# Products of zeros in an attention opening, and another order of loads, transposes and scores for four chunks

## The chip, the cores and the metric

The kernel runs on one core of one Trainium2 chip. The metric is the device time of one execution in microseconds (us), here the median over runs; lower is better. The engines are named as in the profile: PE (TensorE, matrix products), PEld (its weight loads), DVE (VectorE), ACT (ScalarE), POOL (GpSimd) and SP (SyncE, which issues most transfers).

## What is computed

A linear attention with decay over blocks of 64 tokens, whose output goes through a two-layer network. For each batch, head and block:

```python
intra = einsum('bhij,bhjd->bhid', einsum('bhic,bhjc->bhij', qb, kb) * Dmask, vb)
inter = einsum('bhid,bhde->bhie', qb * lam_pow, kv_state)
out[:, :, sl] = intra + inter
kv_state = lam_block * kv_state + einsum('bhsd,bhse->bhde', kb * rev_pow, vb)
...
x = out.transpose(0, 2, 1, 3).reshape(3072, 512)
h = x @ w_in                      # 512 x 2048
return (h / (1 + exp(-h))) @ w_out  # 2048 x 512
```

There are 4 batches, 8 heads, 768 tokens and head size 64; inputs and outputs are float32, and the products are made in bfloat16.

## The kernel before

**Chunks and groups.** The 3072 tokens are cut into 24 chunks of 128 (two blocks of 64 for all 8 heads), two chunks to a group of 256 tokens. A chunk needs q, k and v from memory, scaled by powers of the decay and cast (`prep` on POOL for q and k, `vcast` on ACT for v), then q and k transposed. From chunk 6 on the transposes are made by DMA (`dma_t`, lines 390 and 391), two for each chunk, issued by SP; loads are issued by SP as well (`load_1`, line 232), so both stand in one queue in the order of the program.

**The opening.** Chunks 0 to 3 and the first layer for groups 0 and 1 follow an order written out by hand (`ORDER`), one word for one step: `kc`, `qc`, `vc` scale and cast (last letter: D for DVE, A for ACT, P for POOL); `tk`, `tq` are transposes on PE and `kt`, `qt` copy them out; `s` is the scores, `m` their mask on DVE, `d` the product that adds to the state, `kv` the state's copy to bfloat16, `i` and `o` the two parts of the attention's output, `x` its copy out; `w` casts a piece of w_in, `u` is a part of the first layer and `g` its Silu. Steps of one engine run in the order of the words. `z:n` stands for products of zeros, n units of 256 columns: as long as the state's tile (tag `kv`) isn't open, `op_z` makes them at once, into a tile of the same tag; later it only notes n, for the next tile that `zeros` is called with.

**The groups.** After a middle part for groups 0 and 1, a loop over groups g = 2 to 10 has two stages. First come eight units of the first layer (`ffn1_two`, 8 products of 256 columns each, then a Silu on ACT; two banks of tag `h`, so a unit waits for the Silu two units before it). Then come eight units of the second layer (`downs`, 4 products of 512 columns each; four units make one output of 128 tokens, which DVE copies out, line 648). Two banks `o0` and `o1` take the outputs in turn; `other()` names the one that is not in use by the present output. Between units stand the steps of later chunks: `preps`, `transposes`, `load_qk`, `load_vs`, `vcast`, and `section`, which makes outputs, scores and states of two chunks on PE and lets DVE mask the scores (line 560), add to the state (572) and cast it. In the loop c, d, a, b are the chunks 2g + 2 to 2g + 5. At unit 6 of the second stage a section makes the outputs of c and d and the scores and states of a and b. For chunks 8 and 9 the scores and states were made in a section of their own, ahead of the first layer's last unit in group 3:

```python
if g == 3 and i == 7:
    section((), (c, d), steps(c, d))
ffn1_two(g, i)
```

The loads of q and k ran one chunk ahead of those of v (`c + 7`, `d + 7`), and v of 10 and 11 was issued by ACT (`e=nc.scalar`).

Of the kernel before, what the change touches and what calls it, by code (L numbers as in the profile page):

```python
# [7 lines left out]
F32 = mybir.dt.float32  # L8
# [4 lines left out]
BLK = 128  # L13
# [7 lines left out]
LOADS = "K00 Q00 K01 Q01 V00 V01 K20 Q20 K21 Q21 V20 V21"  # L21

ORDER = """
wl kc:0,0,D,u z:20 qc:0,0,D tk:0,0,o tq:0,0,att kc:0,1,D,s kt:0,0,A qc:0,1,D z:4 qt:0,0,A tk:0,1,h s:0,0,h,o
vc:0,0,P,s kt:0,1,A tq:0,1,att m:0,0,0,D qc:2,0,P vc:0,1,D,u qt:0,1,A s:0,1,h,att kc:2,0,A,u d:0 m:0,0,1,D kv:0,A
tk:2,0,o i:0,0,att,h kt:2,0,A d:1 m:0,1,1,D kv:1,A o:0,0 x:0,0,A m:0,1,0,D vc:2,0,P,s x:1,0,A kc:2,1,D,s tq:2,0,o
tk:2,1,h qt:2,0,D qc:2,1,D s:2,0,o,att m:2,0,0,D i:0,1,o,att tq:2,1,h m:2,0,1,D o:0,1 vc:2,1,D,u d:2,0 kt:2,1,A
qt:2,1,A s:2,1,h,o kv:2,0,A i:2,0,att,att x:0,1,A d:2,1 m:2,1,0,D m:2,1,1,D kv:2,1,A w:0,0,A w:0,1,D o:2,0 i:2,1,h,h
x:2,0,D d:3 o:2,1 x:1,1,D x:3,0,A u:0,0,0,o,o x:3,1,A u:1,0,0,att,att w:1,0,D x:2,1,D w:2,1,D w:1,1,A w:2,0,D w:3,0,D
# [7 lines left out]
def kernel(  # L37
# [10 lines left out]
    nc = tc.nc  # L48
    B, H, S, D = q.shape
# [4 lines left out]
    NP = H // 2  # L54
# [14 lines left out]
    psum = ctx.enter_context(tc.tile_pool(name="psum", bufs=1, space=bass.MemoryType.PSUM))  # L69
# [40 lines left out]
    zero = const.tile([128, 512], BF16, name="zero")  # L110
# [84 lines left out]
    natb, tr, st, kvb, kvps = {}, {}, {}, {}, {}  # L195
    xts = []
    cell = {}

    def zeros(dst):
        fill(dst, cell.pop("z", 0))  # L200

    def fill(dst, n):
        dst = dst if len(dst.shape) == 2 else dst.rearrange({3: "p a b -> p (a b)", 4: "p a b c -> p (a b c)", 5: "p a b c d -> p (a b c d)"}[len(dst.shape)])
        w = dst.shape[1] // 256
        for k in [w] * (n // w) + [1] * (n % w):
            nc.tensor.matmul(dst[:, 0:256 * k], lhsT=zero[:, :BLK], rhs=zero[:, 0:256 * k], start=True, stop=True, skip_group_check=True)
    start = 0
    group_of = {}
    for g, n in enumerate(GROUPS):
# [28 lines left out]
    def load_v(c, e=None):  # L238
        vraw[c] = load_1(v, c, "vf", 6, e)
# [15 lines left out]
    kp, vp, qp, qtp, ktp, sp_, ss_, op_ = {}, {}, {}, {}, {}, {}, {}, {}  # L255
# [25 lines left out]

    def op_s(c, a, *tags):
        sps = [psum.tile([128, 2, 2, 2, 64], F32, name="sp", **bank(t)) for t in tags]
        zeros(sps[0])
        for r in range(2):
            for p in range(2):
                for j, x in ((0, 0), (1, 1), (0, 1), (1, 0)):
                    nc.tensor.matmul(sps[j][half[x], r, p], lhsT=ktp[c][half[j], 2 * a + p, r, half[x]],
                                     rhs=qtp[c][half[j], 2 * a + p, :, half[x]], start=True, stop=True)
        sp_[c, a] = sps  # L290
# [15 lines left out]
    def op_i(c, a, *tags):  # L306
        for x, t in enumerate(tags):
            op_[c + x, a] = psum.tile([128, 2, 2, 64], F32, name="op", **bank(t), padded_shape=[128, NP, 2, 64])
        zeros(op_[c, a])
        last = {}  # L310
        for x, j in ((0, 1), (1, 0), (0, 0), (1, 1)) if c else ((1, 0), (1, 1)):
            for p in range(2):
                last[j] = nc.tensor.matmul(op_[c + x, a][half[j], p], lhsT=kvb[c + x][half[j], 2 * a + p, :],
                                           rhs=qtp[c][half[j], 2 * a + p, :, half[x]], start=(p == 0), stop=False,
                                           skip_group_check=True)
        cell["i", c, a] = list(last.values())
# [18 lines left out]
    def op_d(c, a=None):  # L335
        c0, x = c - c % 2, c % 2
        if c == 0:
            kvps[0] = psum.tile([128, NP, D], F32, name="kv_ps", tag="kv", bufs=1, padded_shape=[128, NP, BLK])
        kv = kvps[0]
        for r in range(2):  # L340
            for p in range(NP) if a is None else (2 * a, 2 * a + 1):
                for j in range(2):
                    h = 2 * (p % 2) + j
                    nc.tensor.matmul(kv[half[j], p, :], lhsT=kp[c0][half[x], p // 2, r, h, :],
                                     rhs=vp[c0][half[x], p // 2, r, h, :],
                                     start=(c == 0 and r == 0 and p == 0), stop=True, skip_group_check=True)
# [248 lines left out]
    hps = {}  # L595

    def ffn1_open(g, i, tag="h"):
        hps[g, i] = psum.tile([128, 512], F32, name="h_ps", **bank(tag))

    def ffn1_mm(g, i, kos):  # L600
        for u in range(2):
            m, a = 2 * i + u, 256 * u
            for ko in kos:
                nc.tensor.matmul(hps[g, i][:, a:a + 256], lhsT=w_in_bf[:, ko, m * 128:(m + 1) * 128], rhs=xt[g][:, ko, :],  # L604
                                 start=(ko == 0 and u == 0), stop=(ko == KO_IN - 1), skip_group_check=True)
# [68 lines left out]
    for word in LOADS.split():  # L674
        a = int(word[2])
        src, dst = {"Q": (q, rawq), "K": (k, rawk), "V": (v, vraw)}[word[0]]
# [5 lines left out]
    def op_u(g, b, h, *tags):  # L682
        if b == 0:
            for i, tag in enumerate(tags):
                ffn1_open(g, i, tag)
            if h == 0:
                zeros(hps[g, 0])
            for i in range(2):
                ffn1_mm(g, i, range(2 * h, 2 * h + 2))
            return  # L690
        ms = (4 * b + 2 * g, 4 * b + 2 * g + 1)
        for m, tag in zip(ms, tags):
            hps["m", m] = psum.tile([128, 512], F32, name="h_ps", **bank(tag))
        if h == 0:
            zeros(hps["m", ms[0]])
        for m in ms:
            for ko in range(2 * h, 2 * h + 2):
                nc.tensor.matmul(hps["m", m], lhsT=w_in_bf[:, ko, m * 128:(m + 1) * 128], rhs=xall[0][:, :, ko, :],  # L698
                                 start=(ko == 0), stop=(ko == KO_IN - 1))
# [13 lines left out]

    def op_z(n):
        if 0 in kvps:
            cell["z"] = n
        else:
            wt = psum.tile([128, NP, BLK], F32, name="warm_ps", tag="kv", bufs=1)
            fill(wt, n)

    table = {
        "qc": op_c(rawq, qp, "qb2", True), "kc": op_c(rawk, kp, "kp"), "vc": op_c(vraw, vp, "vp"),
# [4 lines left out]
    for word in ORDER.split():  # L727
        name, _, args = word.partition(":")
# [6 lines left out]
    def load_qk(*cs, e=None):  # L735
        for c in cs:
            if c < NCHUNK:
                rawq[c] = load_1(q, c, "qf", 4, e)
                load_k(c, e)
                loaded.append(c)  # L740

    def transposes(*cs):
        for c in cs:
            if c < NCHUNK:
                dma_t(c)

    def load_vs(*cs, e=None):
        for c in cs:
            if c < NCHUNK:
                load_v(c, e)  # L750

    def preps(*cs):
        for c in cs:
# [49 lines left out]
    def steps(*cs):  # L803
        return [(c, h) for c, h in [(cs[0] - 1, 1)] + [(c, h) for c in cs for h in range(2)] if c > 5][:-1]

    many = (("h", 2),) * 2 + (("att", 3),) * 2
    for g in range(2, len(GROUPS) - 1):
        c, d, a, b = range(2 * g + 2, 2 * g + 6)
        for i in range(8):
            if g == 2 and i == 4:  # L810
                preps(8, 9)
                load_qk(10)
                transposes(8, 9)
                load_vs(8, 9)
                load_qk(11)
            if g < 4 and i in (4, 5):
                vcast(c + i % 2)
            if g == 3 and i == 7:
                section((), (c, d), steps(c, d))
            ffn1_two(g, i)  # L820
        for i, unit in enumerate(downs(g)):
            if i == 1 and g == 2:
                section((), (c, d), steps(c, d))
            if i == 1 and g > 2:
                vcast(a)
            if i == 2:
                preps(c + 4, d + 4)
                transposes(c + 4, d + 4)
                load_qk(*([12] if g == 2 else []), c + 7)
                load_vs(c + 6, d + 6)  # L830
                load_qk(d + 7)
            if i == 3 and g > 2:
                vcast(b)
            if i == 0 and g == 2:
                load_vs(10, 11, e=nc.scalar)
            if i == 6:
                cs = [x for x in (a, b) if g > 2 and x < NCHUNK]
                section((c, d), cs, steps(*cs) if cs else (), "AD", many[:2] if cs else many, other())
            ffn2(*unit)
    g = len(GROUPS) - 1  # L840
# [35 lines left out]
```

## Time and profile before

| | |
|---|---|
| median of 3 runs | 204.93 us (204.31 to 205.45) |
| the profiled execution | 205.49 us |
| its span, first to last instruction | 203.8 us |
| mean granted PE clock | 0.99 |
| PE busy | 196.6 us (96%) |
| DVE, ACT, POOL busy | 81.5, 90.0, 53.5 us |

All starts below are in us from the first instruction of the profiled execution. A busy PE is not PE at its peak, since products are pipelined; a wait is put down to the work that ended last before it. The granted clock is the share of full speed that PE was given.

### The profile page before, as it was taken

What the parts mean: (1) busy time and instruction counts of PE and PEld (TensorE: products, weight loads), DVE (VectorE), ACT (ScalarE), POOL (GpSimd) and SP (SyncE); (2) the same over time, 40 slices, a digit from 0 to 9 for tenths busy, and PEclk for the clock granted to TensorE, in tenths of its full rate; (3) what the DMA queues carried; (4) which work ended last, traced back from release to release, by engine and by line L of the source; (5) the groups of instructions that cost most, each with busy time, mean ns of one, the idle gap of its engine ahead of it and who ended that gap; (6) DMA issues with size and microseconds to landing.
All of it is one profiled execution on the core that took longest, in us unless ns stands there. A gap on an engine that the chain in (4) does not pass through costs nothing.

```text
span 203.8 us, 6077 instructions
## 1 busy us (share of the span) xinstructions
PE 196.6 (96%) x2636; PEld 130.5 (64%) x2636; DVE 81.5 (40%) x176; ACT 90.0 (44%) x165; POOL 53.5 (26%) x98
## 2 busy tenths in 40 slices
PE   7689999999999899999999999999999999999994
PEld 2368444557747656856856856856856856856854
DVE  1897357294072085515315415414315415412011
ACT  3864973454704731641641641741741741622610
POOL 5240002657062126434425153440400000000000
PEclk9969999999999999999999999999999999999999
DMA  4999999999679949849789594997997601101102
GB/s 107 336 369 408 400 408 270 279 266 211 148 151 164 239 80 246 194 83 227 162 187 201 116 264 91 226 215 169 269 384 152 245 2 55 53 3 55 51 2 103
DMA packets 95579, 38.67 MB, mean 190 GB/s; under 512 B 80960, under 2 KB 88512, under 8 KB 95552
## 3 DMA queue, kind: packets, MB, share of 16 engines
q1 hardware_dynamic: 91248, 37.24, 70.5%
q10 hardware_dynamic: 4304, 1.05, 3.1%
q8 instruction: 20, 0.33, 0.7%
q14 instruction: 7, 0.06, 0.1%
HBM read 27.27 MB, written 6.29 MB: 165 GB/s over the span
## 4 chain that ended last, share of the span: by engine, by line
PE 64%; DMA 2%; SPq 1%; ACT 1%; issue 0%; POOL 0%; DVE 0%
PE o_ps L642 29%; PE h_ps L604 28%; PE op L540 3%; DMA vf<-in_v_dram 2%; PE o_part L662 2%; PE sp L540 1%; SPq L391 1%; PE kv_ps L540 1%; ACT vb L178 0%; POOL kb L364 0%; ACT g L609 0%; DVE ob L182 0%; SPq L390 0%
## 5 line engine op out<-in xcount | busy, mean ns | idle before, releaser
L642 PE MATMUL o_ps<-w_out_bf,g 128*128 128x512 bf16 x368 | 83.8, 379 | 0.0
L604 PE MATMUL h_ps<-xt,w_in_bf 128*128 128x256 bf16 x672 | 75.7, 273 | 1.0 <-ACT g L609 1.0
L604 PEld LDWEIGHTS <-w_in_bf 128*128 128x128 bf16 x672 | 65.6, 98 | 11.2 <-issue 1.1
L609 ACT ACTIVATE g<-h_ps 128x512 bf16<-128x512 f32 x84 | 49.9, 597 | 41.3 <-PE h_ps L604 41.0
L642 PEld LDWEIGHTS <-g 128*128 128x128 bf16 x368 | 34.8, 98 | 38.3
L178 ACT ACTIVATE xt<-op 128x256 bf16<-128x256 f32 (+1 forms) x18 | 8.3, 487 | 46.9 <-issue 34.4
L364 POOL TENSOR_TENSOR qb<-qf,lam_fwd 128x256 bf16<-128x256 f32 x18 | 11.3, 625 | 59.7 <-issue 31.3
L648 DVE COPY ob<-o_ps 128x512 f32<-128x512 f32 x11 | 7.6, 689 | 46.6 <-PE o_ps L642 46.6
L560 DVE TENSOR_TENSOR ss<-sp,mask 128x512 bf16<-128x512 f32 x20 | 12.8, 682 | 14.9 <-PE sp L540 14.9
L182 DVE CAST xt<-op 128x256 bf16<-128x256 f32 (+1 forms) x16 | 8.3, 543 | 21.2 <-PE op L540 20.1
L648 DVE COPY pair<-o_ps 128x512 f32<-128x512 f32 x12 | 8.2, 686 | 16.5 <-PE o_ps L642 16.5
L572 DVE TENSOR_TENSOR total<-total,kv_ps 128x256 f32<-128x256 f32 x33 | 13.6, 414 | 0.1
L364 POOL TENSOR_TENSOR kb<-kf,lam_bwd 128x256 bf16<-128x256 f32 x20 | 12.4, 618 | 4.6 <-DMA kf<-in_k_dram 3.4
L365 POOL TENSOR_TENSOR kb<-kf,lam_bwd 128x256 bf16<-128x256 f32 x20 | 12.5, 625 | 0.0
L178 ACT ACTIVATE vb<-vf 128x512 bf16<-128x512 f32 x20 | 11.6, 622 | 0.9 <-DMA vf<-in_v_dram 0.9
L365 POOL TENSOR_TENSOR qb<-qf,lam_fwd 128x256 bf16<-128x256 f32 x18 | 11.2, 620 | 0.0
L182 DVE CAST kvs<-total 128x256 bf16<-128x256 f32 x33 | 10.5, 319 | 1.1
L698 PE MATMUL h_ps<-xt,w_in_bf 128*128 128x512 bf16 x48 | 10.5, 379 | 0.0
L540 PEld LDWEIGHTS <-vb 64*64 64x64 bf16 x320 | 7.5, 105 | 4.5 <-issue 4.2
L540 PE MATMUL op<-ss,vb 64*64 64x64 bf16 x320 | 9.9, 199 | 0.0
L540 PE MATMUL op<-qt,kvs 64*64 64x64 bf16 x296 | 9.6, 194 | 0.0
L698 PEld LDWEIGHTS <-w_in_bf 128*128 128x128 bf16 x48 | 4.7, 98 | 5.4
(76 smaller groups left out, 126.2 us busy)
## 6 DMA issues: line engine op xcount, KB each, us to landing
kf<-in_k_dram SPq DMA_DIRECT2D x19, 256.0 KB, 4.5
vf<-in_v_dram SPq DMA_DIRECT2D x18, 256.0 KB, 4.2
qf<-in_q_dram SPq DMA_DIRECT2D x17, 256.0 KB, 4.0
pair<-in_moe_w_out_dram SPq DMA_DIRECT2D x8, 512.0 KB, 7.8
pair<-in_moe_w_in_dram SPq DMA_DIRECT2D x6, 512.0 KB, 7.3
out_dram<-pair SPq DMA_DIRECT2D x12, 256.0 KB, 3.9
out_dram<-ob SPq DMA_DIRECT2D x11, 256.0 KB, 3.8
pair<-in_k_dram SPq DMA_DIRECT2D x4, 256.0 KB, 4.5
```

What stands on the lines that cost most here:

```text
L178: nc.scalar.activation(dst, src, AF.Copy)
L182: nc.vector.tensor_copy(dst, src)
L364: eng.tensor_tensor(dst[:, 0::2], src[:, 0::2, ::-1, :], by[:, 0::2, ::-1, :], op=AL.mult)
L365: eng.tensor_tensor(dst[:, 1::2], src[:, 1::2], by[:, 1::2], op=AL.mult)
L540: ins = nc.tensor.matmul(dst, lhsT=lhsT, rhs=rhs, start=start, stop=True, skip_group_check=True)
L560: nc.vector.tensor_tensor(ss, sp.rearrange("k w p q -> k (w p) q"), mask64[:, None, :].to_broadcast([128, len(scores) * NP, D]), op=AL.mult)
L572: nc.vector.tensor_tensor(total[b], old, place(c, h), op=AL.add)
L604: nc.tensor.matmul(hps[g, i][:, a:a + 256], lhsT=w_in_bf[:, ko, m * 128:(m + 1) * 128], rhs=xt[g][:, ko, :], start=(ko == 0 and u == 0), s ...
L609: nc.scalar.activation(gg.rearrange("p u n -> p (u n)"), hps[g, i], AF.Silu)
L642: nc.tensor.matmul(o, lhsT=gt[g, ko][:, mt * BLK:(mt + 1) * BLK], rhs=w_out_bf[:, ko, :], start=(ko == 0), stop=(ko == KO_OUT - 1))
L648: nc.vector.tensor_copy(ob, o)
L698: nc.tensor.matmul(hps["m", m], lhsT=w_in_bf[:, ko, m * 128:(m + 1) * 128], rhs=xall[0][:, :, ko, :], start=(ko == 0), stop=(ko == KO_IN - 1))
```

## The change

Three things are changed.

- In the opening, `z:20` becomes `z:22`, a `z:6` is put ahead of the first transpose of q (`tq:0,0`), a `z:6` ahead of the second scores (`s:0,1`), and a `z:4` ahead of the first transpose of k of chunk 2 (`tk:2,0`). The old `z:4` stays between `tq:0,0` and `tk:0,1`. For the last of them `op_z` is changed: once the state's tile is open, it makes the products at once, 256 columns each and adding, into the second half of that tile, which is now allocated at the same size with two halves.
- In group 2, the loads of v of 8 and 9, q and k of 11, and v of 10 and 11 all stand ahead of the transposes of 8 and 9, and SP issues them; the transposes of 10 and 11 then follow with no loads between. From there each group loads q, k and v of its two chunks after the transposes of the two before (`c + 6`, `d + 6`).
- The section for the scores of 8 and 9 is moved from ahead of unit 7 of the first layer in group 3 to ahead of unit 2 of the second layer.

```diff
-wl kc:0,0,D,u z:20 qc:0,0,D tk:0,0,o tq:0,0,att kc:0,1,D,s kt:0,0,A qc:0,1,D z:4 qt:0,0,A tk:0,1,h s:0,0,h,o
-vc:0,0,P,s kt:0,1,A tq:0,1,att m:0,0,0,D qc:2,0,P vc:0,1,D,u qt:0,1,A s:0,1,h,att kc:2,0,A,u d:0 m:0,0,1,D kv:0,A
-tk:2,0,o i:0,0,att,h kt:2,0,A d:1 ...
+wl kc:0,0,D,u z:22 qc:0,0,D tk:0,0,o z:6 tq:0,0,att kc:0,1,D,s kt:0,0,A qc:0,1,D qt:0,0,A z:4 tk:0,1,h s:0,0,h,o
+vc:0,0,P,s kt:0,1,A tq:0,1,att m:0,0,0,D qc:2,0,P vc:0,1,D,u qt:0,1,A z:6 s:0,1,h,att kc:2,0,A,u d:0 m:0,0,1,D kv:0,A
+z:4 tk:2,0,o i:0,0,att,h kt:2,0,A d:1 ...
...
-    def zeros(dst):
-        fill(dst, cell.pop("z", 0))
-
-    def fill(dst, n):
...
+    def fill(dst, n, start=True):
         w = dst.shape[1] // 256
         for k in [w] * (n // w) + [1] * (n % w):
-            nc.tensor.matmul(dst[:, 0:256 * k], lhsT=zero[:, :BLK], rhs=zero[:, 0:256 * k], start=True, stop=True, skip_group_check=True)
+            nc.tensor.matmul(dst[:, 0:256 * k], lhsT=zero[:, :BLK], rhs=zero[:, 0:256 * k], start=start, stop=True,
+                             skip_group_check=True)
...
         if c == 0:
-            kvps[0] = psum.tile([128, NP, D], F32, name="kv_ps", tag="kv", bufs=1, padded_shape=[128, NP, BLK])
+            both = psum.tile([128, 2, NP, D], F32, name="kv_ps", tag="kv", bufs=1)
+            kvps[0], cell["spare"] = both[:, 0], both[:, 1].rearrange("k p d -> k (p d)")
...
     def op_z(n):
         if 0 in kvps:
-            cell["z"] = n
+            fill(cell["spare"], n, False)
         else:
-            wt = psum.tile([128, NP, BLK], F32, name="warm_ps", tag="kv", bufs=1)
-            fill(wt, n)
+            fill(psum.tile([128, 512], F32, name="warm_ps", tag="kv", bufs=1), n)
...
             if g == 2 and i == 4:
                 preps(8, 9)
                 load_qk(10)
-                transposes(8, 9)
                 load_vs(8, 9)
                 load_qk(11)
+                load_vs(10, 11)
+                transposes(8, 9)
             if g < 4 and i in (4, 5):
                 vcast(c + i % 2)
-            if g == 3 and i == 7:
-                section((), (c, d), steps(c, d))
             ffn1_two(g, i)
         for i, unit in enumerate(downs(g)):
-            if i == 1 and g == 2:
+            if (g, i) in ((2, 1), (3, 2)):
                 section((), (c, d), steps(c, d))
             if i == 1 and g > 2:
                 vcast(a)
             if i == 2:
                 preps(c + 4, d + 4)
                 transposes(c + 4, d + 4)
-                load_qk(*([12] if g == 2 else []), c + 7)
+                load_qk(c + 6, d + 6)
                 load_vs(c + 6, d + 6)
-                load_qk(d + 7)
             if i == 3 and g > 2:
                 vcast(b)
-            if i == 0 and g == 2:
-                load_vs(10, 11, e=nc.scalar)
```

The calls of `zeros` in `op_s`, `op_i` and `op_u` and the argument `e` of `load_vs` are removed with them.

More of the change, by code (lines that the diff above doesn't have):

```diff
@@ L23 @@
 ORDER = """
-wl kc:0,0,D,u z:20 qc:0,0,D tk:0,0,o tq:0,0,att kc:0,1,D,s kt:0,0,A qc:0,1,D z:4 qt:0,0,A tk:0,1,h s:0,0,h,o
-vc:0,0,P,s kt:0,1,A tq:0,1,att m:0,0,0,D qc:2,0,P vc:0,1,D,u qt:0,1,A s:0,1,h,att kc:2,0,A,u d:0 m:0,0,1,D kv:0,A
-tk:2,0,o i:0,0,att,h kt:2,0,A d:1 m:0,1,1,D kv:1,A o:0,0 x:0,0,A m:0,1,0,D vc:2,0,P,s x:1,0,A kc:2,1,D,s tq:2,0,o
+wl kc:0,0,D,u z:22 qc:0,0,D tk:0,0,o z:6 tq:0,0,att kc:0,1,D,s kt:0,0,A qc:0,1,D qt:0,0,A z:4 tk:0,1,h s:0,0,h,o
+vc:0,0,P,s kt:0,1,A tq:0,1,att m:0,0,0,D qc:2,0,P vc:0,1,D,u qt:0,1,A z:6 s:0,1,h,att kc:2,0,A,u d:0 m:0,0,1,D kv:0,A
+z:4 tk:2,0,o i:0,0,att,h kt:2,0,A d:1 m:0,1,1,D kv:1,A o:0,0 x:0,0,A m:0,1,0,D vc:2,0,P,s x:1,0,A kc:2,1,D,s tq:2,0,o
 tk:2,1,h qt:2,0,D qc:2,1,D s:2,0,o,att m:2,0,0,D i:0,1,o,att tq:2,1,h m:2,0,1,D o:0,1 vc:2,1,D,u d:2,0 kt:2,1,A
@@ L197 @@
     cell = {}
-    def zeros(dst):
-        fill(dst, cell.pop("z", 0))
-    def fill(dst, n):
-        dst = dst if len(dst.shape) == 2 else dst.rearrange({3: "p a b -> p (a b)", 4: "p a b c -> p (a b c)", 5: "p a b c d -> p (a b c d)"}[len(dst.shape)])
+    def fill(dst, n, start=True):
         w = dst.shape[1] // 256
         for k in [w] * (n // w) + [1] * (n % w):
-            nc.tensor.matmul(dst[:, 0:256 * k], lhsT=zero[:, :BLK], rhs=zero[:, 0:256 * k], start=True, stop=True, skip_group_check=True)
+            nc.tensor.matmul(dst[:, 0:256 * k], lhsT=zero[:, :BLK], rhs=zero[:, 0:256 * k], start=start, stop=True,
+                             skip_group_check=True)
     start = 0
@@ L283, in op_s @@
         sps = [psum.tile([128, 2, 2, 2, 64], F32, name="sp", **bank(t)) for t in tags]
-        zeros(sps[0])
         for r in range(2):
@@ L308, in op_i @@
             op_[c + x, a] = psum.tile([128, 2, 2, 64], F32, name="op", **bank(t), padded_shape=[128, NP, 2, 64])
-        zeros(op_[c, a])
         last = {}
@@ L685, in op_u @@
                 ffn1_open(g, i, tag)
-            if h == 0:
-                zeros(hps[g, 0])
             for i in range(2):
@@ L693, in op_u @@
             hps["m", m] = psum.tile([128, 512], F32, name="h_ps", **bank(tag))
-        if h == 0:
-            zeros(hps["m", ms[0]])
         for m in ms:
@@ L745, in transposes, with load_vs @@
                 dma_t(c)
-    def load_vs(*cs, e=None):
+    def load_vs(*cs):
         for c in cs:
             if c < NCHUNK:
-                load_v(c, e)
+                load_v(c)
     def preps(*cs):
```

## The prediction

> **What bounds the kernel now.** I read the page first, then the waits, the chain of waits, a table of stretches over the opening, and the timelines of PE, DVE and SP where these pointed. The page says that PE is the bound:
>
> ```profile
> PE 196.6 (96%) x2636; PEld 130.5 (64%) x2636; DVE 81.5 (40%) x176; ACT 90.0 (44%) x165; POOL 53.5 (26%) x98
> ```
>
> So time can only come from PE's gaps, from slow PE stretches, or be lost by new gaps. The waits, over the whole run, name one gap late enough that nothing behind it makes it good, and the chain of waits tells whose it is:
>
> ```profile
> PE h_ps L604 <- ACT g L609: 1.0, 1, 1.0
> ```
> ```profile
> 62.55 2.10 SPq L391
> 64.65 0.05 issue
> 64.70 3.70 DMA vf<-in_v_dram
> 68.40 0.02 issue
> 68.43 0.63 ACT vb L178
> 69.06 0.49 ACT g L609
> 69.55 0.04 issue
> 69.59 1.03 PE h_ps L604 x8
> ```
>
> The loads of v for chunks 8 and 9 stand on SP behind the four transposes of 8 and 9 (55.77 to 64.65). They land at 68.40, ACT's cast waits for them, the next Silu stands behind the cast, and PE waits for the bank that this Silu frees.
>
> The table of stretches, cut at the times when the granted clock changes, shows the other loss. Columns: length, busy us of each engine, granted clock, DMA.
>
> ```profile
> 5.27:8.68 3.41, 2.54 (x36) 1.27 (x34) 2.66 (x5) 3.15 (x5) 0.26 (x1) 1.00 1.11 333
> 8.68:12.10 3.42, 2.28 (x77) 1.80 (x76) 3.42 (x6) 2.64 (x7) 1.83 (x2) 1.00 1.14 343
> 12.10:15.51 3.41, 3.26 (x74) 2.66 (x75) 2.73 (x6) 2.06 (x6) 1.16 (x1) 0.50 1.06 382
> 15.51:18.92 3.41, 3.41 (x91) 3.00 (x85) 2.62 (x6) 2.23 (x6) 0.00 (x0) 1.00 1.06 408
> ```
>
> After the stretch in which PE was busy least (2.28 of 3.42), the clock is halved for 3.41 us. But DVE is busy there nearly throughout, so PE's speed matters only where DVE waits for it:
>
> ```profile
> 13.52 1.29 DVE L294 TENSOR_TENSOR ss<-sp,mask_p 128x512 bf16<-128x512 f32 x2 [0.32 <-PE sp L288]
> 15.58 1.29 DVE L294 TENSOR_TENSOR ss<-sp,mask_p 128x512 bf16<-128x512 f32 x2 [0.44 <-PE sp L288]
> ```
>
> From 17.27 to the end PE has no idle time but that 1.0 us.
>
> **Part 1, products of zeros.** Added are 2, 6, 6 and 4 units of 256 columns (the old 4 keep their place). 64 products of 256 columns take 6.99 us from 80.56, so one is 0.109; one of 512 takes 0.216 (24 in 5.18). Sum 18 x 0.108 = 1.94 us of PE, of which the gaps must hide all:
> - z:22: one more product of 512 before 5.55; the next transpose starts at 5.75 and its reader on ACT not before 6.67. Nothing.
> - the first z:6, 0.65 us, into the gap from tk's end to 6.82, where PE waited 0.67 for DVE. Fits to 0.05.
> - the second z:6, 0.65 us, after the transpose of 8.32, into the 0.69 before 9.40. Fits.
> - z:4, 0.43 us, between d:0 (over at 10.17) and tk:2,0 (10.53). If it may start at once, it ends at 10.6 and costs under 0.1. But it writes the other half of the tile that ACT's copy of the state is reading (10.38 to 10.74). If it must wait for that copy, as the next product into this tile did (10.87), it runs from 10.83 to 11.27. Queued behind it on PE are tk:2,0 (from 10.53 to 11.27), i:0,0, d:1, o:0,0 and tq:2,0 (from 11.75 to 12.25); ACT waits for the first, DVE for the last. I take the wait, since the one row on this tile shows it.
>
> The Trainium skill (PSUM — Partial Sum Buffer, "PSUM bank collisions raise a hardware error") says to guard by bank and not by address: a write beside another engine's read of one bank is an error, whatever the columns. By that the wait is there; no run here shows it for different columns.
>
> What they may bring is the full clock after 12.10. The stretch 8.68 to 12.10 gains about 0.9 us of PE work, from 2.28 to some 3.2 of 3.42, above the 2.54 that kept the clock. With the wait, DVE then runs: copy of tq at 12.64 (12.25 and 0.39 for the transposes), scaling of q 13.02, two masks 13.67, cast 14.88, two masks 15.26. These lengths are those of the rows before (12.18 to 12.52, 12.52 to 13.20, 1.21, 0.38). The scores at full clock are there at 15.23, so the 0.44 is gone. PE's dense work started 1.69 us after those masks (15.58 to 17.27), now at 16.95: gain 0.32. Without the wait the same count starts from 11.75 and gains 0.80. If the clock is halved all the same, tq's 0.5 delay stays and PE's slow scores too: loss 0.65.
>
> What starts earlier must find its weights. The tightest is the last piece of w_out, landed at 41.98 and cast on ACT by 43.15; PE's product with it is at about 43.75. So at most 0.55 us can be carried past it.
>
> **Part 2, SP's queue.** v of 8 and 9, q, k of 11 and v of 10, 11 are now issued ahead of the transposes of 8, from 55.7 on (0.53 to 0.85 us each: until about 60), and not by ACT (59.74 to 61.86, where ACT only delayed an x copy by 0.4 us that PE did not wait for). v of 8 lands near 60, long before its cast at 67.5. PE's 49th product of this stage was due 48 x 0.109 = 5.24 us after 63.22, at 68.46, and came at 69.59: 1.13 lost. The stage before, whose casts waited for nothing, still took 7.22 us (47.48 to 54.70) instead of 6.99: 0.23 for the two casts among the Silus. So gain 1.13 - 0.23 = 0.90.
>
> The transposes of 8 and 9 move back:
>
> ```profile
> 55.77 3.64 SPq L390 DMA_TRANSPOSE qt<-qb  x1
> 59.53 1.20 SPq L391 DMA_TRANSPOSE kn<-kb  x1
> 60.84 1.21 SPq L390 DMA_TRANSPOSE qt<-qb  x1
> 62.55 2.10 SPq L391 DMA_TRANSPOSE kn<-kb  x1
> ```
>
> The first took 3.64 behind four loads. After six more it starts at about 60 and the run of four is issued until about 67.5; with 2.3 us to land, as chunk 7's took with no loads beside them, that is 69 to 70. Their reader, the scores of 8 and 9, moves back by 8 products of 256 and 8 of 512 (0.87 + 1.73 = 2.60): due at 63.22 + 7.22 + 1.73 = 72.2, less 0.32. Cover of 2 us. The transposes of 10 and 11 follow at once, landing near 75 (76.23 before, the last), read after 76.5. The loads of 12 and 13 come next, some 2 us earlier than at 75.18; without the lead the transposes of 12 and 13 stand behind six loads, not eight. Later groups repeat this, and PE had no wait there.
>
> But the move of the scores has a price on DVE, which I take from its rows after the old place (PE's scores at 70.56):
>
> ```profile
> 71.05 1.29 DVE L560 TENSOR_TENSOR ss<-sp,mask 128x512 bf16<-128x512 f32 x2 [6.94 <-PE sp L540]
> ...
> 74.67 0.29 DVE L182 CAST kvs<-total 128x256 bf16<-128x256 f32 x1
> 75.76 0.69 DVE L648 COPY pair<-o_ps 128x512 f32<-128x512 f32 x1 [0.80 <-PE o_ps L642]
> ```
>
> Masks, sums and casts hold DVE until 4.4 us after the scores start. Only then can it copy the output of the group's first token tile, until 5.06 after. That copy used to wait for PE; now it is late. The section of scores of 10 and 11 takes the very bank that it frees (`other()`), and comes 0.67 + 4 x 0.863 = 4.12 us after the scores of 8, its first product into that bank 0.26 later, at 4.38. PE waits 5.1 - 4.4 = 0.7. So part 2 nets 0.90 - 0.70 = 0.20, bounds -0.1 and +0.9.
>
> **Sum.** 0.32 + 0.20 = 0.52 us off the profiled 205.49 (span 203.8 and 1.7 around it), which lies 0.56 above the median of 204.93 and at the top of the runs. Off the median: 204.4.
>
> **The rivals.**
> - Nothing is handed back at the copy, since DVE gets through sooner or the bank is free. For it: DVE has been idle 6.94 us before. Against: its eleven instructions are in order. Then 0.90 + 0.32 = 1.22: 203.7, and 203.5 if the zeros needn't wait for ACT (0.55 carried).
> - The clock is halved all the same, or one stretch later, because zeros count little, or because the stretch from 12.10 at full speed has fewer busy us (about 2.2 of issue) and is judged low itself. In the first case +0.65 - 0.20: 205.4; in the second dense work runs at half speed, +1.2 - 0.2: 205.9. Against the first: the ten products of zeros at the start ran 0.43 us apart (weight loads at 1.66, 2.08, 2.51), and the clock's records are at 1.00 from 5.27, after nothing but zeros. The Trainium skill (TensorE: Matmul & The Clock Gate, "HAM oscillation — how this bites in real kernels") asks only for no idle gap over some 3.4 us; by that rule zeros in gaps of 0.4 to 0.7 us change no clock, and this is where the time would go. The trace disagrees: it halved with no gap over 0.69.
> - Slower: the transposes of 9 land after PE reaches the scores. Between 59.5 and 62.6, with loads beside them, they took 5 to 6.4 us to land. If so here (issue 67.2, landing 73.6), PE waits 73.6 - 71.9 = 1.7, DVE's price stays, and the end is 1.7 - 0.5 = 1.2 later: 206.1. It decides from a landing after 71.9. Against it: no loads are issued beside them now.
>
> **How the numbers follow.** Forecast 0.40, first rival 0.31, clock 0.16, late transposes 0.13. About 0.5% (1.0 us) is what a measurement of this kernel can tell from no change. Faster by more: the first rival and the 0.09 of the forecast with a larger opening, 0.40. Within: the rest of the forecast and half of the clock's case, 0.39. Slower: 0.21. The range runs from the first rival with 0.3 for the opening's bounds, 203.2, to the clock's later case, 206.0; the forecast's own is 203.9 to 204.9.
>
> **What would show it.** Right: a clock of 1.00 from 5.3 on; PE's first h_ps near 16.9; no wait of PE on ACT near 68; a wait of PE sp on DVE's copy of 0.7 near 76. Wrong: a stretch at 0.50, a wait of PE on kn near 72, or PE's sp after that copy without a wait.

## The result and the profile after

The changed kernel takes 206.08 us (median of 22 runs, 205.12 to 207.78), the kernel before 205.24 us beside it (22 runs, 204.27 to 206.50): a ratio of 1.0054, 95% interval 1.0030 to 1.0079. It is slower by about 1 us, where 0.5 us faster was forecast, and lies just outside the range that ended at 206.0. (Ratios are taken over all the executions and not from the two medians, so the two can differ a little.)

The profiled execution took 206.59 us, with a span of 204.9. The times at which stages start show where it went:

| start, us | before | after | later by |
|---|---|---|---|
| first `h_ps` (end of the opening) | 17.27 | 18.78 | 1.51 |
| first layer, group 2 | 47.48 | 49.20 | 1.72 |
| first layer, group 3 | 63.22 | 64.94 | 1.72 |
| first layer, group 4 | 80.40 | 81.76 | 1.36 |
| end | 203.78 | 204.88 | 1.10 |

So the opening lost 1.5 us, the stretch behind it 0.2 more (its first products still ran at the halved clock of the table below), and the stretch with the new queue gave 0.36 back. The last 0.26 is no more than such stretches differ: from group 4 to the end the profiles of either loop take 123.1 to 123.5. The waits of PE over the whole run (us in total, times, longest us) show both parts of the change:

```profile
PE o_ps L638 <- issue: 2.1, 13, 0.2
...
PE tq L266 <- DVE qb L250: 0.9, 1, 0.9
PE kv_ps L202 <- ACT kvc L178: 0.6, 1, 0.6
PE sp L536 <- DVE pair L644: 0.4, 1, 0.4
```

The first row is no lost time: at such places this profile has records of seven products where the one before has eight. The 1.0 us on ACT's Silu is gone. In its place stand a wait of PE for DVE's scaling of q, the wait of the new zeros for ACT's copy, and the wait for DVE's copy of an output.

**The opening.** The same table of stretches as for the kernel before, cut again at the steps of the granted clock (length, busy us of each engine, granted clock, DMA):

```profile
5.61:9.02 3.41, 3.38 (x40) 1.69 (x40) 2.69 (x5) 3.10 (x5) 0.49 (x1) 1.00 1.15 344
9.02:12.44 3.42, 2.71 (x80) 2.11 (x78) 3.32 (x6) 2.01 (x5) 1.59 (x2) 1.00 1.12 332
12.44:15.85 3.41, 1.98 (x61) 1.55 (x64) 3.04 (x5) 1.98 (x7) 1.04 (x1) 1.00 1.07 381
15.85:19.26 3.41, 3.41 (x91) 3.08 (x91) 2.97 (x8) 1.94 (x7) 0.00 (x0) 0.50 1.05 408
```

The zeros fill PE up to 12.44, and the clock is full in the stretch behind. But in that stretch PE is busy only 1.98 of 3.41, and the halved clock comes one stretch later, over the start of the dense work. The timelines of DVE and POOL in the kernel before, and of PE, DVE and POOL in the changed one, say why PE is empty there. Before:

```profile
12.52 0.68 DVE L253 TENSOR_TENSOR qb<-pair,lam_fwd 128x512 bf16<-128x512 f32 x1
```
```profile
12.94 1.16 POOL L253 TENSOR_TENSOR vp<-pair,lam_bwd 128x512 bf16<-128x512 f32 x1 [1.25 <-DMA pair<-in_v_dram]
```

After:

```profile
10.90 0.60 PE L202 MATMUL kv_ps<-zero 128*128 128x256 bf16 x4 [0.62 <-ACT kvc L178]
```
```profile
12.81 0.42 DVE L182 COPY qtp<-tq 128x512 bf16<-128x512 bf16 x1 [0.47 <-PE tq L266]
13.15 1.52 DVE L250 TENSOR_TENSOR qb<-pair,lam_fwd 128x512 bf16<-128x512 f32 x1
```
```profile
13.08 1.04 POOL L250 TENSOR_TENSOR vp<-pair,lam_bwd 128x512 bf16<-128x512 f32 x1 [1.29 <-DMA pair<-in_v_dram]
```
```profile
14.73 0.40 PE L266 MATMUL tq<-ident,qb 128*128 128x128 bf16 x4 [0.92 <-DVE qb L250]
```

The last zeros wait 0.62 for ACT; DVE's scaling of q, which started at 12.52 and took 0.68 before, starts at 13.15, 0.07 behind POOL's scaling of v, and takes 1.52; PE stands 0.92 behind it.

**The groups.** DVE's row of work and PE's first product behind it, at the section of the second stage of group 3:

```profile
78.10 0.29 DVE L182 CAST kvs<-total 128x256 bf16<-128x256 f32 x1
78.30 0.68 DVE L644 COPY pair<-o_ps 128x512 f32<-128x512 f32 x1
```
```profile
78.45 0.21 PE L536 MATMUL kv_ps<-vb,kb 64*64 64x64 bf16 x2
79.04 0.22 PE L536 MATMUL sp<-qt,kn 64*64 64x64 bf16 x2 [0.37 <-DVE pair L644]
```

No product of PE starts between 78.45 and 79.04, 0.59 us. The queue of SP:

```profile
61.52 1.92 SPq L229 DMA_DIRECT2D vf<-in_v_dram  x2
63.55 2.62 SPq L386 DMA_TRANSPOSE qt<-qb  x1
...
74.13 1.21 SPq L387 DMA_TRANSPOSE kn<-kb  x1
```

The transposes start at 63.55 and the last one is issued at 74.13; it landed at 78.09.

### The profile page after: what moved, and what is told of

The parts are those of the page before. It is cut to its first block, busy times and chain, and to the rows that moved or that the text cites. A ratio compares the mean times of both kernels' runs of the same rounds, so it can differ in the third digit from the quotient of the medians.

```text
span 204.9 us, 6078 instructions
## 1 busy us (share of the span) xinstructions
PE 195.6 (95%) x2621; PEld 131.5 (64%) x2647; DVE 82.0 (40%) x176; ACT 89.4 (44%) x165; POOL 53.4 (26%) x98
## 4 chain that ended last, share of the span: by engine, by line
PE 89%; DVE 3%; DMA 2%; SPq 2%; issue 2%; ACT 1%
PE o_ps L638 36%; PE h_ps L600 36%; PE h_ps L690 5%; PE op L536 3%; DMA pair<-in_k_dram 2%; SPq L221 2%; PE sp L536 2%; PE o_part L658 2%; PE kv_ps L536 1%; DVE qb L250 1%; DVE total L568 1%; PE op L318 1%; DVE kvs L182 1%; DVE ss L556 1%; PE op L308 1%
## 5 line engine op out<-in xcount | busy, mean ns | idle before, releaser
L638 PE MATMUL o_ps<-w_out_bf,g 128*128 128x512 bf16 x343 | 79.9, 379 | 2.6 <-issue 2.1
L568 DVE TENSOR_TENSOR total<-total,kv_ps 128x256 f32<-128x256 f32 x33 | 13.6, 413 | 0.1
```

What stands on the lines that cost most here:

```text
L568: nc.vector.tensor_tensor(total[b], old, place(c, h), op=AL.add)
L638: nc.tensor.matmul(o, lhsT=gt[g, ko][:, mt * BLK:(mt + 1) * BLK], rhs=w_out_bf[:, ko, :], start=(ko == 0), stop=(ko == KO_OUT - 1))
```

## Experiments: the opening

Each kernel was timed in turn with the kernel before, whose median was 205.62, 205.46, 205.19 or 204.99 in the four sets of runs, so kernels of different sets are compared by their ratios alone. "h" is the start of the first `h_ps` in the profile. A profile is of one execution, which can lie far from the median: 205.31 against 206.21 for the queue and the scores alone, 207.38 against 206.12 for the scaling one step sooner, 206.97 against 205.66 for the finer cut in the kernel before.

**Without the last four units of zeros.** The changed kernel, with one word left out:

```diff
-z:4 tk:2,0,o i:0,0,att,h ...
+tk:2,0,o i:0,0,att,h ...
```

> The changed kernel without the last z:4 (ahead of tk:2,0); all else as changed. Theory A (the last zeros wait for ACT's copy, hold up the transpose of q of chunk 2 by 0.5 us, push DVE's scaling of q beside POOL's scaling of v, where it took 1.52 instead of 0.68 us, and leave PE so idle that the clock halves in the dense work from 15.85): the DVE scaling is back to 0.7 us, PE's first h_ps starts near 16.5 to 17.3, and the time is 0.6 to 1.4 us under the kernel before (ratio 0.993 to 0.997). Rival B (the products of zeros as a whole cost, wherever they stand): first h_ps stays above 18, ratio stays near 1.005. Rival C (the loss comes from the new order of loads, transposes and scores): ratio above 1.003 though h_ps starts near 17.

Measured: 205.86 us, ratio 1.0014 (0.9983 to 1.0044). In the profile DVE's scaling starts at 12.47 and takes 0.68, the records show no halved stretch, and h is 17.89. So in the profile the last zeros are what costs most in the opening. But h did not come to 16.5 to 17.3, nor the ratio under 1: the full clock brought nothing against the 17.27 of before, since PE stood still inside one step, waiting for nothing that the trace names.

```profile
15.26 0.36 PE L318 MATMUL op<-ss,vp 64*64 64x128 bf16 x12
17.02 0.25 PE L318 MATMUL op<-ss,vp 64*64 64x128 bf16 x4 [1.39 <-issue]
```

**The zeros alone.** The kernel before with the first part of the change:

```diff
-wl kc:0,0,D,u z:20 ...
+wl kc:0,0,D,u z:22 ...
...
-            cell["z"] = n
+            fill(cell["spare"], n, False)
```

> Part 1 alone: all the products of zeros of the change, with the loads, transposes and scores of the kernel before. Theory A and rival B: slower than before by the opening's loss, 1.72 us at the start of group 2 in the profile after, a little less in executions whose clock stays full: ratio 1.004 to 1.009. Rival C: no slower than before, ratio under 1.001.

Measured: 206.09 us, ratio 1.0023 (0.9991 to 1.0054), less than expected; h 17.75, DVE's scaling 1.45 us, PE's wait on the Silu 1.0 as before. This profiled execution was not halved, so the 1.5 us of the table above is one of two cases; both are slower than 17.27. Counted from the first transpose of k to h, which leaves out a late start, the opening of before takes 11.52 to 11.91 in four profiles, this kernel 12.06, the scores one unit sooner (below; the same zeros, not halved either) 12.12, and the changed kernel in the table 12.92. So in these profiles the zeros cost some 0.2 to 0.6 without the halving there, and the halved stretch some 0.8 more.

**DVE's scaling one step sooner.** The changed kernel, with two words exchanged:

```diff
-tk:2,1,h qt:2,0,D qc:2,1,D s:2,0,o,att ...
+tk:2,1,h qc:2,1,D qt:2,0,D s:2,0,o,att ...
```

> The changed kernel with DVE's scaling of q (qc:2,1) ahead of its copy of the transposed q (qt:2,0), so that it is over before POOL's scaling of v starts at 13.0. Theory A alone (the loss is that scaling beside POOL, 1.5 instead of 0.7 us): the scaling takes 0.7 us, PE's wait for it (0.9) goes, first h_ps comes 0.6 to 0.9 us sooner than in the zeros-only run, at about 17.0, and the time is within 0.2% of the kernel before or under it. Theory D (code arrives at 16.5 to 17.0): the scaling takes 0.7 us too, but PE then stands before its 448th, first h_ps comes at 17.5 to 17.9, the pause moves from 13.5 to 15.5 or later, and the ratio to before is 1.002 to 1.005.

Measured: 206.12 us, ratio 1.0038 (1.0002 to 1.0073). The scaling is back to 0.69 (at 12.61) and the clock stays full, but PE waits 0.6 for POOL's v until 15.49 and no product starts for 0.52 before 17.26; h is 18.19, in an execution that started its first transpose 0.46 later than before (6.21 and 5.75). In this execution, removing DVE's delay alone didn't bring the opening forward.

**The last zeros in a bank of their own.** The changed kernel; the four units go into the bank of the output that PE fills next, and don't wait for ACT:

```diff
 def op_i(c, a, *tags):
     ...
+    fill(op_[c, a].rearrange("p a b c -> p (a b c)"), cell.pop("z", 0))
...
-            fill(cell["spare"], n, False)
+            cell["z"] = n
```

> The changed kernel, whose last four units of zeros go into the bank of the attention's output that PE fills next, and not into the spare half of the state's bank that ACT is reading: they stand one step later, between the transposes of k of chunk 2 and the first output, and wait for nobody. PE still does their 0.43 us. Theory (the wait for ACT's copy, 0.6 us, is what pushes DVE's scaling of q under POOL's scaling of v): the transposes of q of chunk 2 start at 11.8 to 12.1 instead of 12.4, DVE's scaling starts by 12.8 and takes 0.7 to 0.9 us instead of 1.5, PE has no gap over 0.5 us near 13.6, and the first h_ps product comes at 17.3 to 18.0 instead of 18.8: ratio 1.001 to 1.002. Rival (it is the 0.43 us of products, wherever they stand): the scaling stays near 1.5 us, the gap near 13.6 stays near 1.1 us, and the ratio stays at 1.004 to 1.006.

Measured: 206.13 us, ratio 1.0037 (1.0006 to 1.0068). The opening came out nearly as the theory said: h 17.41, the scaling at 12.99 and 0.68 long, no gap near 13.6, and no halved stretch in any of 12 executions. Counted from the first transpose, h comes after 11.46. DVE now comes 0.14 ahead of POOL, and POOL pays:

```profile
12.99 0.68 DVE L250 TENSOR_TENSOR qb<-pair,lam_fwd 128x512 bf16<-128x512 f32 x1
```
```profile
13.13 1.44 POOL L250 TENSOR_TENSOR vp<-pair,lam_bwd 128x512 bf16<-128x512 f32 x1 [1.25 <-DMA pair<-in_v_dram]
```

So it is the wait and not the 0.43 us of products. The ratio did not follow. In the profile a later wait opened:

```profile
77.56 0.22 PE L537 MATMUL sp<-qt,kn 64*64 64x64 bf16 x2 [0.37 <-DVE pair L645]
...
78.83 0.22 PE L537 MATMUL sp<-qt,kn 64*64 64x64 bf16 x2 [0.95 <-DMA kn<-kb]
```

It is the landing that differs here, not PE's place: with the queue and the scores alone (below) PE came to this section at the same 77.56, and found `kn` of chunk 11 landed at 77.74; here it landed at 78.79.

**More PE instructions ahead.** The kernel without the last zeros, whose other zeros are cut finer (128 columns in the first step, 256 elsewhere):

```diff
-        w = dst.shape[1] // 256
-        for k in [w] * (n // w) + [1] * (n % w):
-            nc.tensor.matmul(dst[:, 0:256 * k], ...
+        w = 128 if n == 22 else 256
+        for _ in range(256 * n // w):
+            nc.tensor.matmul(dst[:, 0:w], ...
```

> The changed kernel without the last z:4, and the remaining products of zeros cut narrower at the same total of columns: the 22 units of the warm-up as 44 products of 128 columns, the other three as products of 256. That is 82 PE instructions more ahead of the rest of the opening for the same streaming time. Theory D (PE's code comes in blocks of 256 instructions; the block that begins near PE's 448th product or weight load arrives only 1.3 to 1.5 us after a 16 KB code transfer that starts at 14.1 to 14.6 behind the loads, so at 16.5 to 17.0 whatever PE did before): the pause falls again between PE's 447th and 448th, which is now 82 instructions earlier in the program, it is longer (some 2.3 instead of 1.6 us), and PE's first h_ps comes 1.7 to 2.0 us after the 448th instead of 0.87: 18.4 to 19.0. Rival: the pause in the run without the last zeros was a wait of those products on other engines; then it stays at the same products, and the first h_ps stays within 0.3 of 17.9.

Measured: 206.09 us (8 runs), ratio 1.0048 (1.0013 to 1.0083). Theory and rival both failed in the profile: the pause is gone and h is 17.17. One 16 KB transfer on the queue named "instruction" came at 10.51 to 11.39, where the other kernels have it ending at 14.8 to 16.8. Yet the time is no better. The profiled execution, 205.46, is one of the two shortest of the eight; the other six took 205.88 to 207.36, and no trace shows what they waited for.

**The same finer cut in the kernel before.**

```diff
-        w = dst.shape[1] // 256
...
+        w = 128 if n == 20 else 256
+        for _ in range(256 * n // w):
```

> The kernel before, whose 20 units of zeros ahead of the first transpose are 40 products of 128 columns and not 10 of 512: the same columns, 60 more PE instructions. Theory (PE's code comes in blocks of 256 instructions, and the block it lacked at 16.5 was asked for only when PE had started on the block before it, by which time the loads of w_in had filled the queues): the third block is now asked for before 10, its transfer is over by 11.5 and not 15.1, nothing is waited for near PE's 448th instruction, and the first h_ps product comes at 16.7 to 17.1 (DVE's last masks of the opening end at 16.87) instead of 17.27. That is at most 0.5 us: ratio 0.997 to 0.999. Rival (the code's arrival bounds nothing in this kernel, the half clock alone does): first h_ps at 17.2 to 17.4, ratio 1.000. A second rival, from the kernel with narrow products and more zeros, which timed 1.005 although its profile was no longer: something else makes the narrow form dear, and this kernel too is at 1.003 or above.

Measured: 205.66 us, ratio 1.0003 (0.9969 to 1.0038). The transfer started at 12.44, 1.7 us sooner than before, but took 2.56 and not 0.96 and was over at 15.00 (before: 15.11). So it was not early in the sense that counts, the kernel didn't do what it was built for, and says nothing on whether an early transfer helps. The pause stands again behind PE's 447th instruction (weight loads and products counted), though 32 products and their loads were added ahead of it (30 in the first step, 2 in the old `z:4`) and the step there is another one: it follows the count of instructions, not a step. It ends at 15.98; h is 18.30, after a further 0.67 behind a late load of v and a first transpose 0.55 later than before, at a clock full from 4.62 on.

## Experiments: the queue and the scores

Here the measure is the time from group 2's first product to group 4's, 32.92 us before and 32.56 after. The kernels of the first part give further executions of either loop: 32.90 and 32.99 with the loops of before (zeros alone, finer cut), and 32.79, 33.77, 32.55, 33.69 with the changed loops (without the last zeros, scaling sooner, more instructions, own bank).

**The queue and the scores alone.** The kernel before with the other two parts:

```diff
-                transposes(8, 9)
                 load_vs(8, 9)
                 load_qk(11)
+                load_vs(10, 11)
+                transposes(8, 9)
...
-            if i == 1 and g == 2:
+            if (g, i) in ((2, 1), (3, 2)):
```

> Parts 2 and 3 alone: the new order of loads, transposes and scores, with the opening of the kernel before. Theory A and rival B: faster than before by what the traces show from group 3 on, 0.36 us from group 3 to group 4 and 0.26 after, together 0.3 to 0.6 us: ratio 0.997 to 0.9985. Rival C: slower, ratio 1.003 or more.

Measured: 206.21 us, ratio 1.0037 (1.0003 to 1.0072). Its profiled execution is no slower (span 203.6, 32.65 from group 2 to 4, the wait for the copy 0.59). But it took 205.31 and is one of five executions of 205.00 to 205.39; the other seven took 206.07 to 208.32. So the profile stands for the short executions alone. The other profiles of the changed loops (the changed kernel and four of the first part) say what can differ: of all six, four have only the wait for the copy, and two (scaling sooner, own bank) have a wait of 1.0 for `kn` of chunk 11 as well. The mean of the six is 33.00, against 32.92: over these profiles the part gains nothing. That this wait is what the seven longer executions had is not shown.

**The scores one unit sooner.** The changed kernel, with the section ahead of unit 1:

```diff
-            if (g, i) in ((2, 1), (3, 2)):
+            if (g, i) in ((2, 1), (3, 1)):
```

> The changed kernel with the section for the scores of 8 and 9 ahead of unit 1 instead of unit 2 of the second layer in group 3. By my step on DVE's copy: DVE is through its masks, sums, casts and the copy before the section of outputs starts, the PE wait on that copy (about 0.6 us in the profile after) goes, and the transposes of 9, landed at 71.2 there, are in time for scores at 73.1: 0.5 to 0.6 us less than the changed kernel, ratio to before near 1.002. Rival: the transposes of 9 are late or the wait only moves, ratio stays near 1.005.

Measured: 206.74 us, ratio 1.0057 (1.0027 to 1.0087); 33.36 from group 2 to 4. The wait for the copy is gone, and PE waits 0.8 for `kn` of chunk 11 instead, which landed at 79.33. So the rival's case came: taking away one wait shows the next.

**The loads of v first, nothing else.** The kernel before, with one line moved:

```diff
-                transposes(8, 9)
                 load_vs(8, 9)
+                transposes(8, 9)
```

> The kernel before with one edit: the loads of v of 8 and 9 ahead of the transposes of 8 and 9 on SP; opening, other loads, place of the scores unchanged. My step on the cast: PE's wait of 1.0 us near 68.5 goes and 0.23 for the two casts stays, so 0.9 us less from group 3 to group 4; with the scores left at their old place DVE's copy is in time, so none of it is handed back: span near 202.9, ratio 0.994 to 0.997. Rival: the transposes of 9, issued 1.4 us later, land after the scores are due at about 69.6, and PE waits for them instead: ratio 0.998 to 1.002, with a PE wait on kn.

Measured: 205.53 us, ratio 0.9998 (0.9967 to 1.0029); 32.94. The first layer of group 3 takes 8.23 instead of 8.89, and the gain is lost again at 77.73: PE waits 0.7 for `kn` of chunk 11, landed at 78.62 and not 76.23 (0.83 of this is that group 2 itself began later, at 48.31). Two loads ahead of the transposes are enough to hand it back.

**Two pairs of loads exchanged.** The kernel before; no queue gets more:

```diff
                 transposes(8, 9)
-                load_vs(8, 9)
+                load_vs(10, 11)
...
             if i == 0 and g == 2:
-                load_vs(10, 11, e=nc.scalar)
+                load_vs(8, 9, e=nc.scalar)
```

> The kernel before, in which two pairs of loads change places: v of 8 and 9 are issued by ACT in group 2, where v of 10 and 11 were, and v of 10 and 11 by SP behind the transposes of 8 and 9, where v of 8 and 9 were. No queue gets more or less. Theory (in the changed kernel the 0.9 us gained at the cast went to two new waits, DVE's copy, because the scores moved, and chunk 11's transposes, because loads were put ahead of them; here nothing is moved or put ahead): v of 8 and 9 land at 65 to 67.2, ahead of the cast at 67.5; v of 10 and 11 at 68.4 and 69.3, ahead of theirs at 73; PE's wait on ACT near 68 is gone, the first layer of group 3 takes 8.0 us with the scores in it and not 8.9, DVE's copy and chunk 11's transposes make PE wait for nothing, and group 3 to group 4 takes 16.3 us instead of 17.2. Ratio 0.995 to 0.997. Rival (PE meets another wait of about the same length whatever is done, since every landing near 76 to 78 is tight): group 3 to group 4 at 17.0 to 17.3 and the ratio at 0.999 to 1.001.

Measured: 204.46 us (12 runs) against 204.99, ratio 0.9988 (0.9963 to 1.0013). The profile is as expected, the ratio is not (0.995 to 0.997): span 202.8, 31.89 from group 2 to 4, 1.03 less than before. PE's groups run through:

```profile
63.43 6.38 PE L604 MATMUL h_ps<-xt,w_in_bf 128*128 128x256 bf16 x56
69.74 0.45 PE L540 MATMUL sp<-qt,kn 64*64 64x64 bf16 x32
70.02 0.46 PE L540 MATMUL kv_ps<-vb,kb 64*64 64x64 bf16 x32
70.41 1.05 PE L604 MATMUL h_ps<-xt,w_in_bf 128*128 128x256 bf16 x8
71.30 5.34 PE L642 MATMUL o_ps<-w_out_bf,g 128*128 128x512 bf16 x24
76.57 0.22 PE L540 MATMUL op<-ss,vb 64*64 64x64 bf16 x2
```

`kn` of chunk 11 landed at 74.81, and neither it nor DVE's copy is waited for.

**The loads of v by POOL.** The kernel before:

```diff
+                load_vs(8, 9, e=nc.gpsimd)
                 preps(8, 9)
...
-                load_vs(8, 9)
```

> The kernel before, in which POOL issues the loads of v of 8 and 9, ahead of its scaling of q and k of 8, where it was idle from 50.3 to 55.8; SP has two transfers fewer between 64.7 and 65.9. Theory as in the kernel beside it: v of 8 and 9 land before 60, PE's wait on ACT near 68 is gone, the transposes of chunk 11 start 1 us earlier and land by 75.3, so nothing is handed back: group 3 to group 4 in 16.3 us, ratio 0.995 to 0.997. Rival (the two loads, moved to 50 to 55 us, stand beside the transposes of 7 and the loads of 9 and 10 in the transfer engines and make those late; POOL's scaling of 8 starts later and the transposes of 8 behind it): the transposes of 8 land after 63 and 9's after 69, chunk 11's after 77, and PE waits for kn of 11 by 0.5 to 1.0 us: ratio 0.999 to 1.002.

Measured: 204.67 us against 204.99, ratio 1.0003 (0.9982 to 1.0025); again 31.89 from group 2 to 4, `kn` of chunk 11 at 74.86, no wait of PE on either. h is 18.78 in its profiled execution, the longest of 12, whose clock was granted in full only from 14.10. Two independent ways of mending the cast give the same 1.03 in the profile. In the times that is 0.5 us and 0.3 us by the medians, both inside the intervals: by these runs neither version is proven faster than before, though the exchanged loads are the best candidate.

## Why the prediction was wrong

**The opening, "gain 0.32" (failed).** In the profile it was a loss of 1.51. Two steps of the working fell.

- *"These lengths are those of the rows before."* The wait of the last zeros came as forecast (0.6), and put DVE's scaling at 13.15 (13.02 forecast). But POOL's scaling of v starts near 13.0 (12.94 before), and beside it DVE's takes 1.52, not 0.68. Whichever of the two starts first keeps its length: POOL 0.07 ahead, DVE 1.52 and POOL 1.04; DVE 0.14 ahead, DVE 0.68 and POOL 1.44. The term was short by 0.84. What the later one loses is the overlap less 0.13 to 0.14: 0.84 of 0.97 and 0.40 of 0.54. The kernel before showed it already, on POOL: started within DVE's scaling, with an overlap of 0.26, its row took 1.16. The Trainium skill (SBUF — State Buffer, "Who interferes with whom") says that a DVE instruction with two inputs in SBUF and a GpSimd one that reads SBUF contend for what they share, as for an exclusive lock, and that the order of issue decides who blocks; these rows agree with it.
- *"What they may bring is the full clock after 12.10."* The full clock brings little here. Beside the experiments the kernel before ran 106 times: 75 executions have the full clock already (mean granted clock 0.998 or more), with a median of 205.13; the 31 others (0.992 or less) have 205.61. By set the difference is 0.41, 0.32, -0.15 and 0.47. So zeros that always kept the clock could save, as an estimate, some 0.48 x 31/106 = 0.14 us. The exchanged loads, whose opening is that of before at a full clock from 6.82 on, have h at 17.49: PE pauses 0.95 us behind its 447th instruction. The 1.69 us from the masks to the dense work was taken as fixed and is not.

**The clock's rival, its later case (came true).** "The stretch from 12.10 at full speed has fewer busy us (about 2.2)" is 1.98 of 3.41, and dense work ran at half speed, as that case said; it was priced at 205.9. But in 13 of 22 executions of the changed kernel the clock is full, and their median, 205.78, is 0.65 above that of before at a full clock (205.13, in other sets of runs, whose medians go from 204.75 to 205.31). The other nine have 207.53. So the loss is made of both: of what is there at a full clock too (DVE's delay, 1.45 to 1.54 for the scaling in all three profiles with these zeros and this order, and the handing back), and of a halved clock in nine. That it lay over dense work is on record for the profiled one alone; the 1.75 between the two medians is about half of 3.41, as it would be there.

**The zeros' wait (right).** It was taken from the one row on this tile, and 0.62 was measured, with the zeros and the copy in different columns of one tile. The Trainium skill's rule that the prediction cited for it (PSUM — Partial Sum Buffer, "PSUM bank collisions raise a hardware error"), to guard by bank and not by address, agrees with that wait; what would happen without it no run shows. The clock rule that the prediction cited from the Trainium skill (TensorE: Matmul & The Clock Gate, "HAM oscillation — how this bites in real kernels"), no idle gap over some 3.4 us, does not cover what came: the clock was halved at 15.85 with no gap between PE's starts over 1.14 us in the stretch ahead.

**Part 2, 0.90 gained at the cast (near).** The first layer of group 3, now without the scores, took 7.43 in this profile, 7.44 in three others of the changed loops and 7.22 in two (7.22 forecast); before it took 8.89 - 0.67 = 8.22 without them. So the gain is 0.8 to 1.0, and with 0.59 handed back at the copy the profile's 0.36 stands beside the 0.20 forecast.

**"PE waits 5.1 - 4.4 = 0.7" (right).** It is 0.57 to 0.59 in all six profiles of the changed loops.

**"Landing near 75" (failed).** The transposes were to start near 60 and did at 63.55: the six loads ahead began at 57.59 and not 55.7, and took until 63.44 and not 60. Those of chunk 11 landed at 78.09. In this execution PE was itself late, by the opening's loss, and they were there. In the six profiles of these loops they landed at 76.54 to 79.54; in two, at 78.79 and 79.54, PE waited 1.0. The third rival (late transposes) had the right mechanism one pair of chunks too early: chunk 9's landed at 71.21, 2.8 us ahead of its scores. Its own sum was 206.1, which the stated range left out; that the measured 206.08 falls on it is luck.

**The two parts by their times.** The queue and the scores alone have 1.0037, the zeros alone 1.0023, both 1.0054: within the intervals the two losses add up. So part 2, forecast to gain 0.20, loses by its times (1.0003 to 1.0072), though the profile of the changed kernel shows a gain; what the longer executions waited for is not shown.

What stays open: what made seven of twelve executions of the queue and the scores alone, and six of eight of the finer cut with the early code transfer, longer than the one profiled (spans 203.6 and 203.75). One profile for each can't show it.

## What to carry to other kernels

When a wait is taken away by putting work ahead in a queue, follow every item behind it to its own due time: here 0.9 us came back first at a copy and then at a transpose, and in the profiles it was kept only where nothing more stood ahead of the transposes, by an exchange of loads or by another engine's queue. When a step moves, lay it against what the other engines do at its new time; a row's duration holds only beside the same neighbours. And before something is bought with added work (here a full clock), look in several executions whether it isn't there already, and what it was worth.

## What was not expected of the hardware

**The place of the halved clock.** The records change in steps of 3.41 us from a start that differs between executions (full from 5.27 before, from 6.82 with the exchanged loads, from 14.10 with POOL's loads). Five profiles have the opening of before: with full clock from 5.22, 5.27 and 5.52 it is halved from 12.05, 12.10 and 12.35, with full clock from 6.82 and 14.10 it is not. So the same opening seems to be halved or not by where those steps fall; no run set them. With the exchanged loads no stretch is as empty as the 2.28 that was followed by the halving before, and none is halved:

```profile
6.82:10.24 3.42, 2.66 (x62) 1.77 (x62) 3.09 (x5) 2.58 (x5) 1.04 (x1) 1.00 1.11 334
10.24:13.65 3.41, 2.77 (x76) 1.97 (x80) 3.41 (x7) 2.66 (x7) 1.72 (x2) 1.00 1.14 364
13.65:17.06 3.41, 2.52 (x95) 2.04 (x95) 3.35 (x8) 2.37 (x6) 0.47 (x1) 1.00 1.05 401
```

But PE's busy share alone doesn't decide it: with the finer cut in the kernel before, a stretch with 1.70 of 3.41 (from 4.62) was followed by full clock, and one with 2.32 (from 11.62, the scores one unit sooner) too, where one with 2.33 (from 8.93, the loads of v first) was followed by the half.

**A pause at one count of instructions.** In eight profiles PE pauses by 0.37 to 1.61 us ahead of its 447th or 448th instruction, whatever the step there, and goes on 1.0 to 1.6 us after a transfer of 16 KB on the instruction queue ended (without the last zeros: 15.57 and 17.02; exchanged loads: 15.17 and 16.74). In four others it comes to that instruction only 1.4 to 2.1 us after that end, and there is no pause. In the one kernel where the transfer ended at 11.39, and PE came there at 14.87, there is none either. That PE waits for its code is read from this, not shown by an experiment: the kernel meant to bring the transfer forward moved its start and not its end. The Trainium skill (Runtime: NRT & Kernel Launch, "Instruction fetch mechanics") has code arrive in blocks of 16 KiB and calls the cost mostly hidden; in this opening, beside the loads of w_in, it seems not to be.
